# A delta-rule recurrence and a low-rank mixer in one kernel: PSUM as four double banks, regrouped transposes and joins, another load order

## The chip, the cores and the metric

The kernel runs on one core of a Trainium2 chip. The core has a matrix engine (TensorE, PE in the profile), three engines for elementwise work (VectorE or DVE, ScalarE or ACT, GpSimd or POOL), a queue engine for transfers (SyncE or SP) and 16 DMA engines. The metric is the device time of one execution in microseconds. The kernel before takes 720.28 us, the median of three runs (718.12 to 721.35).

## The reference

All data are float32 with 4 batches, 8 heads, 768 steps and head size 48. The first block is the delta rule, one state of 48 x 48 for each batch and head:

```
k_n = k / (norm(k) + 1e-6)
for t in range(S):
    y[t]  = q[t] @ state
    v_old = k_n[t] @ state
    state = state + beta[t] * outer(k_n[t], v[t] - v_old)
```

The eight heads of y are laid side by side (x: 4 x 768 x 384), and the second block is a mixer with rank 32 and an inner width of 1536:

```
u   = x + ((x.T @ U) @ V).T        # over the 768 steps
out = u + relu(u @ w_ch1) @ w_ch2
```

The mixer's inputs U, V, w_ch1 and w_ch2 come as float64.

## The kernel before

**Units and chunks.** The 768 steps are cut into 12 chunks of 64. A unit is six chunks of one batch for all heads, so there are eight units, two to a batch. The data of a unit live in one of two slots in SBUF, so the loads of unit n wait until the recurrence of unit n - 2 has ended (`load`, L252).

**Grams** (`grams`, L359). K and then Q of a unit are transposed on TensorE, two chunks at a time, four transposes into one PSUM bank (`turn`, L367). `products` (L375, L382) multiplies the transposed K with itself and with the transposed Q; the K products are copied by ScalarE (L393), the Q products masked by VectorE (L397).

**Inverse.** Within a chunk the rule needs the inverse of a unit-triangular 64 x 64 matrix. `blocks` (L428) brings the 32 x 32 diagonal blocks into a layout with one block on each partition: unit 0 through TensorE (L465), the others by a round trip through DRAM (L479, L486). There VectorE solves them column by column, with a product (L497) and a subtraction (L503) per column. `split` says whether a block is solved whole (31 columns) or as two halves of 16 (15 columns, twice as many systems at once); units 0 and 1 are split. The result goes back (L522, or L544 and L549). `joins` (L565) puts the blocks together with small matmuls. For a split unit there is an inner join (L579, L598) that joins the halves of 16 to blocks of 32, on all four quarters of 32 rows. The outer join (L621, L638) joins the blocks of 32 to 64, and its matmuls read and write two row quarters. `diagonals` (L652) copies the finished diagonal blocks with GpSimd (L658) and clears the lower ones (L664).

**Recurrence** (`recur`, L673). For each of a batch's 12 chunks: state times K (L704), the first part of y (L715), the right side on VectorE (L725), inverse times right side (L734), a copy z by ScalarE (L743), the state's increment (L749), the second part of y (L759), the new state on VectorE (L772). `put` (L681) copies y to X.

**Weights** (`load_weights`, L801). 27 slices of float64 are loaded as pairs of 32-bit words by GpSimd's queue and turned into float32 by four VectorE instructions and one more on ScalarE (L834 to L862). GpSimd adds and subtracts the halves of w_ch2 (`sums`, L794).

**Mixer.** `front` (L875) computes u for 256 rows, and transposes it (L885, L899, L903, L907). `wide` (L918) does the first layer (L972) with its relu on ScalarE (L928), sums on GpSimd (L944, L951), and the second layer in seven products (L1005), each added to X by VectorE (L957) and stored. There are three such groups to a batch.

**Order.** All parts are Python generators. `run` (L125) is a planner: it keeps a modelled clock for each engine, a modelled state of PSUM and of the loads' landing (`landing`, L106), and emits at each point the ready operation of the highest priority (the second argument of `begin`; a small number is first) that doesn't start more than `HOLD` = 0.15 us after the soonest. The emitted order is each engine's program order. The recurrences of batches 1 to 3 have priority 59, later units' grams and blocks 68 and more, the mixer's matmuls 95. PSUM's eight banks are handed out by name: `pair` has three double banks (0-1, 2-3, 6-7), `one` two single banks (4, 5), and when the mixer starts, 6 and 7 become its two banks `mix` (L921).

## Time and profile before

| | |
|---|---|
| median of the runs | 720.28 us (718.12 to 721.35) |
| the profiled execution | 725.51 us, span 723.7 us |
| TensorE busy, share of the span | 637.3 us, 88% |
| VectorE | 377.1 us, 52% |
| GpSimd | 215.0 us, 30% |
| ScalarE | 182.9 us, 25% |
| mean granted TensorE clock | 0.884 |
| moved by DMA | 44.27 MB, mean 61 GB/s |
| chain that ended last | TensorE 52%, VectorE 29%, DMA 8% of the span |

The profile is of one execution. Busy time is the time in which an engine had at least one instruction under way; matmuls overlap, so the mean duration of one is longer than busy time divided by count. A stage's row gives the stretch, its length, then busy time and instruction count of TensorE, of its weight loads, of VectorE, ScalarE and GpSimd, and at last the granted clock, the DMA share and GB/s. A timeline row gives start, duration, engine, line, operation, operands and count, and in brackets how long the engine had been idle and what it waited for. A group's row gives busy time, the mean of one instruction in ns, and the idle time before. In the lines, `<-` reads "written from".

### The profile page before, as it was taken

What the parts mean: (1) busy time and instruction counts of PE and PEld (TensorE: products, weight loads), DVE (VectorE), ACT (ScalarE), POOL (GpSimd) and SP (SyncE); (2) the same over time, 40 slices, a digit from 0 to 9 for tenths busy, and PEclk for the clock granted to TensorE, in tenths of its full rate; (3) what the DMA queues carried; (4) which work ended last, traced back from release to release, by engine and by line L of the source; (5) the groups of instructions that cost most, each with busy time, mean ns of one, the idle gap of its engine ahead of it and who ended that gap; (6) DMA issues with size and microseconds to landing.
All of it is one profiled execution on the core that took longest, in us unless ns stands there. A gap on an engine that the chain in (4) does not pass through costs nothing.

```text
span 723.7 us, 23375 instructions
## 1 busy us (share of the span) xinstructions
PE 637.3 (88%) x10344; PEld 540.5 (75%) x10344; DVE 377.1 (52%) x925; ACT 182.9 (25%) x399; POOL 215.0 (30%) x281
## 2 busy tenths in 40 slices
PE   5667688659598899999798999999799999999998
PEld 4556576528486688789686887798677887989997
DVE  7577768799958631249678240469494111201001
ACT  3232235325121241331112322421113112020110
POOL 7326341233450250130350511123604302231412
PEclk9965555559798999999979999999799799999999
DMA  9731439852060231342211321521402000000000
GB/s 155 126 92 28 120 84 184 183 125 67 0 122 24 45 73 36 74 88 56 54 36 34 74 56 39 109 48 36 90 24 45 3 24 2 23 0 23 1 23 22
DMA packets 132964, 44.27 MB, mean 61 GB/s; under 512 B 126336, under 2 KB 129408, under 8 KB 132864
## 3 DMA queue, kind: packets, MB, share of 16 engines
q1 hardware_dynamic: 127776, 30.20, 21.2%
q0 software_dynamic: 3488, 12.29, 6.5%
q8 instruction: 81, 1.33, 0.8%
q10 hardware_dynamic: 1600, 0.30, 0.3%
q14 instruction: 19, 0.16, 0.1%
HBM read 32.54 MB, written 10.22 MB: 59 GB/s over the span
## 4 chain that ended last, share of the span: by engine, by line
PE 52%; DVE 29%; DMA 8%; issue 4%; SPq 3%; ACT 1%; POOL 1%; ACTq 0%; DVEq 0%; POOLq 0%
PE P L1005 18%; PE P L972 16%; DVE prod L497 11%; DVE xt L503 10%; PE P L638 2%; PE P L621 2%; SPq L269 2%; PE P L382 2%; DMA slot<-in_q_dram 2%; PE P L899 2%; PE P L367 2%; PE P L734 2%; DMA scr<-xt 2%; DMA wide<-in_moe_w_ch_dram 1%; PE P L704 1%
## 5 line engine op out<-in xcount | busy, mean ns | idle before, releaser
L972 PE MATMUL P<-ut,w_sb 128*128 128x256 f32 x864 | 213.3, 396 | 0.0
L972 PEld LDWEIGHTS P<-ut,w_sb 128*128 128x128 f32 x864 | 161.8, 194 | 24.8 <-issue 0.6
L1005 PE MATMUL P<-w_sb,hs 128*128 128x192 f32 x720 | 129.5, 333 | 0.0
L1005 PEld LDWEIGHTS P<-w_sb,hs 128*128 128x128 f32 x720 | 118.3, 192 | 3.2
L944 POOL TENSOR_TENSOR S<-hs 128x384 f32<-128x384 f32 x24 | 24.7, 1030 | 256.6 <-ACT hs L928 256.6
L957 DVE TENSOR_TENSOR X<-X,P 128x192 f32<-128x192 f32 x84 | 29.5, 351 | 133.4 <-PE P L1005 133.2
L497 DVE TENSOR_TENSOR prod<-gs,xt 128x112 f32<-128x112 f32 (+21 forms) x216 | 86.6, 401 | 6.0
L503 DVE TENSOR_TENSOR xt<-xt,prod 128x112 f32<-128x112 f32 (+21 forms) x216 | 84.2, 390 | 8.0 <-DVE prod L497 0.7
L928 ACT ACTIVATE hs<-P 128x512 f32<-128x512 f32 x72 | 43.0, 597 | 167.6 <-PE P L972 157.5
L1005 PE MATMUL P<-w_sb,S 128*128 128x192 f32 x288 | 56.5, 350 | 5.3 <-POOL S L944 5.3
L1005 PEld LDWEIGHTS P<-w_sb,S 128*128 128x128 f32 x288 | 50.6, 204 | 6.7 <-POOL S L944 5.8
L367 PE MATMUL P<-ident,slot 128*128 128x128 f32 x192 | 37.9, 331 | 9.1 <-DMA slot<-in_q_dram 7.7
L685 ACT COPY X<-P 64x192 f32<-64x192 f32 x96 | 30.1, 314 | 53.4 <-PE P L759 52.8
L658 POOL COPY slot<-zc 32x384 f32<-32x384 f32 x64 | 33.0, 516 | 27.4 <-DVE zc L606 21.3
L382 PE MATMUL P<-slot 48*64 48x64 f32 x1536 | 39.0, 250 | 2.4 <-DVE slot L397 0.7
L382 PEld LDWEIGHTS P<-slot 48*64 48x64 f32 x1536 | 32.6, 159 | 9.6 <-issue 3.4
L743 ACT COPY z<-P 128x192 f32<-128x192 f32 x48 | 15.2, 317 | 89.7 <-PE P L734 89.4
L367 PEld LDWEIGHTS P<-ident,slot 128*128 128x128 f32 x192 | 26.2, 166 | 13.7 <-issue 9.8
L772 DVE TENSOR_TENSOR s<-s,P 128x192 f32<-128x192 f32 x40 | 14.0, 349 | 40.7 <-PE P L749 40.3
L704 PEld LDWEIGHTS P<-s,slot 48*64 48x64 f32 x704 | 16.7, 155 | 24.7 <-DVE s L772 9.4
L734 PEld LDWEIGHTS P<-rhs,slot 64*64 64x64 f32 x704 | 16.9, 155 | 23.3 <-DVE rhs L725 13.1
L734 PE MATMUL P<-rhs,slot 64*64 64x48 f32 x704 | 22.6, 250 | 12.4 <-DVE rhs L725 12.4
(102 smaller groups left out, 769.9 us busy)
## 6 DMA issues: line engine op xcount, KB each, us to landing
wide<-in_moe_w_ch_dram POOLq DMA_DIRECT2D x24, 384.0 KB, 4.0
slot<-in_k_dram SPq DMA_DIRECT2D x84, 72.0 KB
slot<-in_q_dram SPq DMA_DIRECT2D x64, 72.0 KB
out_dram<-X SPq DMA_DIRECT2D x24, 192.0 KB
slot<-in_v_dram SPq DMA_DIRECT2D x48, 72.0 KB
scr<-slot SPq DMA_DIRECT2D x28, 96.0 KB
gs<-scr SPq DMA_DIRECT2D x28, 96.0 KB
scr<-xt SPq DMA_DIRECT2D x28, 96.0 KB
```

The costliest lines, as they stand in the source:

```text
L367: nc.tensor.transpose(p_t[:, c, j], t[:, c0 + c, 2 * j : 2 * j + 2].rearrange("p s d -> p (s d)"), ident)
L382: nc.tensor.matmul(p_g[half(g ^ (par * i)), par, c, j], kq[rows, c0 + c, j, 0, half(g)], kq[rows, c0 + c, j, i, half(g)], start=True, stop ...
L497: nc.vector.tensor_tensor(out=prod, in0=gb[:, :, j : j + 1, j + 1 :].to_broadcast([128, split, m, w]), in1=xb[:, :, 0:m, j : j + 1].to_bro ...
L503: nc.vector.tensor_tensor(out=xb[:, :, 0:m, j + 1 :], in0=xb[:, :, 0:m, j + 1 :], in1=prod, op=ALU.subtract,)
L658: nc.gpsimd.tensor_copy(out=heads(pg[quarter(i)])[:, at, a : a + BK], in_=zc[quarter(i), at])
L685: nc.scalar.copy(x[half(c % 2), c // 2, 4 * D * g : 4 * D * (g + 1)].rearrange("p (j r d) -> p r j d", r=2, d=D), states(p_y)[half(g)],)
L734: nc.tensor.matmul(states(p_c)[half(g ^ par), par, j], zt[half(g), par, cu, j], rhs[half(g), 2 * par + j], start=True, stop=True,)
L928: nc.scalar.activation(hs[:, fs[0] : fs[1] + 1 : fs[1] - fs[0]], p_f, ACTF.Relu)
L944: nc.gpsimd.tensor_tensor(out=to, in0=a, in1=c, op=how)
L957: nc.vector.tensor_tensor(out=to, in0=to, in1=p, op=ALU.add)
L972: nc.tensor.matmul(p_f[:, fs.index(f)], w1_sb[:, t, f * 128 : (f + 1) * 128], ut[:, t], start=(t == 0), stop=(t == KT - 1),)
L1005: nc.tensor.matmul(p_o, a[:, f], w2_sb[:, w, f], start=(first and f == 0), stop=(f == HF - 1), skip_group_check=True,)
```

## The change

- PSUM is handed out as four double banks, `pair` = (0-1, 2-3, 4-5, 6-7); the single banks are gone, and all users take a pair. Banks 6 and 7 still become the mixer's.
- `grams` is two parts, one for K and one for Q, that run apart. A transpose group takes six chunks of one head pair into two banks; products and evictions are by six chunks too. Loads report after each half of the heads.
- The outer join's matmuls use all four row quarters: one head's product sits on the upper, the other's on the lower rows. Their number is the same.
- Units 2 and 3 are split as well (`n < 4`). For unit 2 and later, the diagonal blocks are moved by DMA and not copied by GpSimd: for units 2 and 3 from SBUF, for later ones straight from DRAM. For units 0 and 1, ScalarE takes two of the eight copies.
- The second part of y is its own part, `result`, with a priority just after the recurrence's. z and the state have three buffers each.
- The weights wait for unit 0's seed, the Q load of unit 0 loses its early place, beta is loaded and turned in two parts, the square of the first K goes to GpSimd, and the memsets at the start are divided differently.
- In the planner, the landing is estimated one microsecond later, the starting clocks of VectorE and GpSimd are changed, and priorities under 13 may hold an engine for 0.7 us.

```diff
-    BANK = dict(pair=[0, 2, 6], one=[4, 5], mix=[6, 7])
+    BANK = dict(pair=[0, 2, 4, 6], mix=[6, 7])
...
-        return max(1.9, state["hw"] + 1.4 - state["now"])
+        return max(2.0, state["hw"] + 2.4 - state["now"])
...
-                    hold = HOLD if i[0] < 90 else SWITCH
+                    hold = 0.7 if i[0] < 13 else HOLD if i[0] < 90 else SWITCH
...
+    nc.vector.memset(P[:, :, 0:256], 0.0)
...
-    nc.vector.memset(P[:, 0:4], 0.0)
-    nc.vector.memset(P[:, 4:8], 0.0)
-    nc.vector.memset(gs, 0.0)
+    nc.gpsimd.memset(gs, 0.0)
...
+    nc.gpsimd.memset(zc, 0.0)
...
-        yield need(("rec", n - 2))
+        yield need(("rec", n - 2), *[("x", b - 1, UC * hf + c) for c in range(UC)])
...
+        if n == 0:
+            yield op("pool", 2.1)
+            nc.gpsimd.tensor_tensor(
+                out=ksq, in0=kn[:, :, :, 0:D], in1=kn[:, :, :, 0:D], op=ALU.mult
+            )
...
+        def turn(t, j, i):
+            x = yield op("pe", 0.66, "F", take="pair")
+            p_t = pair(x)[:, :, 0:384].rearrange("p b (c t) -> p b c t", c=3)
+            for c in range(UC):
+                nc.tensor.transpose(
+                    p_t[:, c // 3, c % 3],
+                    t[:, c, 2 * j : 2 * j + 2].rearrange("p s d -> p (s d)"),
+                    ident,
+                )
...
+        def products(j, i):
+            x = yield op("pe", 0.7, "Q", take="pair")
+            p_g = pair(x)[:, :, 0:384].rearrange("p r (c t) -> p r c t", c=UC)
...
-        split = 2 if n < NU else 1
+        split = 2 if n < 4 else 1
...
-                yield op("sp", 0.52)
-                nc.sync.dma_start(
-                    out=zc[quarter(i)], in_=scr2[i].rearrange("q s t -> s q t")
-                )
+                blk, a = scr2[i].rearrange("q s t -> s q t"), BK * (i % 2)
+                if split == 2 or i % 2 == 0:
+                    yield op("sp", 0.52)
+                    nc.sync.dma_start(out=zc[quarter(i)], in_=blk)
+                if split == 1:
+                    yield op("sp", 0.52)
+                    nc.sync.dma_start(out=heads(pg[quarter(i)])[:, :, a : a + BK], in_=blk)
...
                 for g in range(2):
-                    rows = quarter(2 * g + 1)
+                    up, low = quarter(2 * g), quarter(2 * g + 1)
                     nc.tensor.matmul(
-                        p_x[quarter(2 * g), e - 12 * r],
-                        pg[rows, a, c, j, 0:BK],
-                        zc[rows, e],
-                        start=True,
-                        stop=True,
+                        p_x[up, c], pg[low, r, c, 0, 0:BK], below(c, 0, g), start=True, stop=True
+                    )
+                    nc.tensor.matmul(
+                        p_x[low, c], pg[up, r, c, 1, BK:L], above(c, 1, g), start=True, stop=True
                     )
...
                 for g in range(2):
-                    rows = quarter(2 * g)
+                    up, low = quarter(2 * g), quarter(2 * g + 1)
                     nc.tensor.matmul(
-                        p_v[rows, e - 12 * r], zn[rows, e], xz[rows, e], start=True, stop=True
+                        p_v[up, c, 0], above(c, 0, g), xz[up, r, c], start=True, stop=True
+                    )
+                    nc.tensor.matmul(
+                        p_v[up, c, 1], xz[low, r, c], below(c, 1, g), start=True, stop=True
                     )
...
+            if n < NU:
+                for i in range(4):
+                    a = BK * (i % 2)
+                    to, of = heads(pg[quarter(i)])[:, at, a : a + BK], zc[quarter(i), at]
+                    if i < 2 or r == 0:
+                        yield op("pool", 0.5)
+                        nc.gpsimd.tensor_copy(out=to, in_=of)
+                    else:
+                        yield op("act", act(384))
+                        nc.scalar.copy(to, of)
+            elif split == 2:
+                for i in range(4):
+                    a = BK * (i % 2)
+                    yield op("sp", 0.55)
+                    nc.sync.dma_start(
+                        out=heads(pg[quarter(i)])[:, at, a : a + BK], in_=zc[quarter(i), at]
+                    )
+                yield op("sp", 0.0, lat=2.5)
...
+        def result(c, y, z):
+            n, cu = NU * b + c // UC, c % UC
+            _, _, _, qk, _, _, _, _ = units[n]
+            if c == 0:
+                y = yield op("pe", 0.35, "Q", take="pair")
+            else:
+                yield op("pe", 0.35, "Q")
+            p_y = pair(y)[:, :, 0 : 2 * D]
+            for j, par, g in heads:
+                at = half(g ^ par)
+                nc.tensor.matmul(
+                    states(p_y)[half(g), par, j],
+                    qk[at, par, cu, j],
+                    z[at, 2 * par + j],
+                    start=(c == 0 and j == 0),
+                    stop=(j == 1),
+                    skip_group_check=True,
+                )
+            emitted(("y", b, c))
+            yield from put(c, y, p_y)
...
+            yield need(("y", b, c - 3)) if c > 2 else []
             yield op("act", act(192), give=[("pair", xc)])
-            z = small.tile([128, 4, D], FP32, name="z")
+            z = small.tile([128, 4, D], FP32, name="z", bufs=3)
             nc.scalar.copy(z.rearrange("p (r j) d -> p r (j d)", r=2), p_c)
+            begin(result(c, y, z), 2 if b == 0 else 60)
...
+        yield need(("seeded", 0))
         begin(start(0), 22)
...
-        begin(load_beta(), 4)
+        begin(load_beta(0), 12)
+        begin(load_beta(1), 16)
...
-            begin(grams(n), place_of(n))
+            begin(grams(n, 0), place_of(n))
+            begin(grams(n, 1), place_of(n) + 3)
...
-            begin(load(n, "q", (0, 1)), 21 + 4 * n if n else 5)
+            begin(load(n, "q", (0, 1)), 21 + 4 * n)
```

## The prediction

> **What bounds the kernel now.** I read four kinds of view: the page's slices, the busy time by stage, the order of instructions at the stage borders, and the groups with shapes kept apart. The slices (40 of 18.1 us) come first:
>
> ```profile
> PE   5667688659598899999798999999799999999998
> DVE  7577768799958631249678240469494111201001
> PEclk9965555559798999999979999999799799999999
> ```
>
> TensorE is full from about the twelfth slice on. Before that it works in gaps, at half clock, while VectorE carries 5 to 9 tenths. I cut the span where the last product of the first batch's recurrence ends (146.5 us), where the second layer starts (195), and where the last recurrence has ended (610.5). Columns: stretch, its length, busy time of the five engines, granted clock, DMA:
>
> ```profile
> 0.00:146.50 146.50, 101.07 (x3296) 86.73 (x3296) 105.28 (x260) 47.56 (x103) 56.40 (x98) 0.65 0.60 121
> 146.50:195.00 48.50, 31.86 (x231) 23.17 (x227) 46.56 (x86) 15.38 (x28) 20.52 (x19) 0.78 0.26 68
> 195.00:260.00 65.00, 58.37 (x1063) 48.52 (x1063) 42.15 (x115) 14.36 (x37) 20.19 (x28) 0.90 0.28 57
> 260.00:610.50 350.50, 335.96 (x5166) 280.75 (x5164) 169.35 (x431) 91.71 (x208) 89.99 (x113) 0.96 0.24 51
> 610.50:723.70 113.20, 110.02 (x601) 101.31 (x600) 13.80 (x35) 13.93 (x25) 27.93 (x25) 1.00 0.04 15
> ```
>
> From 195 us on TensorE is busy 58.4 + 336.0 + 110.0 = 504.4 us of 528.7: idle 24.3. So the end is the moment S at which the second layer starts, plus TensorE's remaining work, plus its idle time. S is 195 now. What sets S is in TensorE's order of instructions:
>
> ```profile
> 183.20 1.45 PE L899 MATMUL P<-tt,v_sb 128*128 128x384 f32 x4
> 193.66 1.54 PE L907 MATMUL P<-ident,X 128*128 128x128 f32 x6 [9.01 <-DVE X L903]
> 195.00 5.71 PE L1005 MATMUL P<-w_sb,hs 128*128 128x192 f32 x24
> ```
>
> The nine idle microseconds are VectorE's: the addition L903 stands behind the substitution of unit 2 (L497, L503), and so did the weight conversion, whose last piece (L862) ended at 183.6; the weight sums on GpSimd (L798) followed until 191.6. In 140 to 200 us the two substitution lines take 18.3 + 16.4 = 34.7 us of VectorE for this one unit. Unit 1, solved as two half-size systems, took 4.3 + 4.4 = 8.7 between 60 and 140.
>
> The small matmuls, by group:
>
> ```profile
> L638 PE MATMUL P<-xz,zn 32*32 32x32 f32 x768 | 21.1, 219 | 1.9 <-issue 1.0 <-ACT xz L630 0.9
> ...
> L621 PE MATMUL P<-zc,slot 32*32 32x32 f32 x768 | 20.3, 216 | 0.0
> ...
> L598 PE MATMUL P<-xz,zn 32*32 32x16 f32 x384 | 6.7, 210 | 7.4 <-issue 7.4
> ...
> L579 PE MATMUL P<-zc,slot 32*32 32x16 f32 x384 | 6.2, 210 | 1.2 <-issue 1.2
> ```
>
> Busy time over count: 27 ns a record for the joins on two row quarters (L621, L638), 16 to 17 ns for those on four (L579, L598).
>
> [...] the second pair also has half the columns. [...] twelve records of L1005 take 1.95 us alone, 2.15 between tile groups, so 0.2 us for an interleaved group. [...]
>
> ```profile
> 37.12 2.23 DVE L497 TENSOR_TENSOR prod<-gs,xt 128x128 f32<-128x128 f32 x1
> ...
> 37.08 2.12 POOL L354 TENSOR_TENSOR slot<-slot,norm_v 128x1152 f32<-128x1152 f32 x1 [2.05 <-DMA slot<-in_v_dram]
> ```
>
> The first is 0.29 us where GpSimd rests.
>
> **The change, part by part: S.** (1) Units 2 and 3 are solved in halves. Of the 34.7 us of unit 2, 20.5 lay before 184; 8.7 take their place: -11.8 on VectorE before the weights end. Added there: two more transposes (0.56 each) and two corrections L606 (0.42 each): +2.0. (2) One memset of PSUM instead of two (1.77), that of gs (0.94) goes to GpSimd: -2.7. (3) Masks by 384 instead of 256 columns: 18 of 0.417 = 7.5 for units 0 to 2 become 12 at about 0.55 (the 384-column additions of L903) = 6.6: -0.9. Sum of 1 to 3: -13.4. (4) The gather for unit 0 was ready at 27.5, but L474 ran at 30.47, behind the norm of unit 1, whose K landed at 25.5. Weights that load after the seed (15.9 us) leave K1 the queues, and the loads' landing is planned later: -3. The late start of the weights costs nothing: the two pieces converted by 18.8 fit into VectorE's idle time from 18.9 to 26.7, and if they don't, 2.5 us a piece (68.7 us for 27). (5) L903 is no longer behind the long substitution: L1005 follows the sums (191.6) and not 195: -3.4. Together -19.8: **S = 175**. Low end 5 us of gain: if recurrence or loads pace the weights, only (2) and part of the others remain; high end 28, if all 20.5 us leave.
>
> At nothing on this path: the square of K0 on GpSimd (2.1 us by L354, against 1.16 on ScalarE) feeds a factor ready at 15.7, needed at 27.5; the memsets on GpSimd, about 2 us ahead of the beta loads, whose first use is at 9.5, some 4 us after landing; the copies of unit 0 shared by ScalarE and VectorE; two evictions of 768 columns for three of 512 on ScalarE (0.317 us at 192 columns and 0.586 at 512 give 0.80: 1.6 us for 1.76, on an engine a quarter busy); the loads' new wait for the x of the same half a batch earlier, whose products end within a step (under 0.7 us) of the recurrence that they waited for anyway. If that cover goes, each costs its own 1 to 2 us.
>
> **TensorE after S: 504.4.** (a) Unit 2's join (209.0 to 212.4: 3.4) and the rest of unit 3's Q grams (after 200: 3.3) now fall before S, where TensorE idles: -6.7. Unit 2's new inner join lies there too. (b) The outer joins keep their number, 192 records a unit, but alternate over four row quarters, with 192 columns evicted for 384 at the first step. Units 3 to 7 take 25.4 us now; at 16.1 ns they would take 5 x 192 x 0.0161 = 15.5: -9.9. Bounds: nothing, if instruction supply limits it (after bursts at 16 ns the trace shows idle "issue" times of 1.4 to 2.3 us), to -12. (c) Unit 3's inner join: half of 6.2 + 6.7: +6.5. (d) Transposes by six: as many records, but 8 groups a unit for 12; units 4 to 7 save 16 x 0.2 = -3.2. (e) The second y product keeps its place after the state product if both are ready, at no cost; placed alone, 36 x 0.2 = +7.2. I take 0. Sum: 504.4 - 6.7 - 9.9 + 6.5 - 3.2 = **491.1**.
>
> **Idle after S: 24.3.** Unit 3's substitution in 218 to 250 (11.2 + 12.0 us) becomes 8.7, so VectorE frees PSUM sooner: I take 3 off the 6.6 idle between 195 and 260. Two stalls come from GpSimd's memset, queued ahead of the sums L944 and waiting for a DMA:
>
> ```profile
> 359.44 0.98 POOL L445 MEMSET xt<- 128x1056 f32 x1 [11.94 <-DMA scr<-xt]
> ...
> 512.00 0.98 POOL L445 MEMSET xt<- 128x1056 f32 x1 [10.59 <-DMA scr<-xt]
> ```
>
> TensorE waited 5.3 us for L944. The wait stays in the code; the later landing estimate and unit 4's earlier start may move it; I take half, 2.6. Idle: **18.7**, bounds 8 and 30.
>
> GpSimd loses 48 diagonal copies of 0.516 (24.8 us); SP gains 8 issues for units 2 and 3 and 2 for each later one, at about 0.6. Unit 2's now wait on SP for the corrected blocks, and loads and stores stand behind them. SP's loads are 28 x 0.62 = 17 us of some 75 a unit, so 5 us are hidden; uncovered, that unit's next load slips by them. DMA runs at a quarter of its capacity there.
>
> Sum: 175 + 491.1 + 18.7 = 684.8 span. The profiled execution was 1.8 over its span and 5.2 over the median shown, so **about 682 us** in the median's terms.
>
> **What PSUM's new division decides.** Unit 4's last K transposes ran at 268.97, its products at 298.84, right after the recurrence's last step: by the code, the two pairs were in the recurrence's hands.
>
> ```profile
> 268.97 0.66 PE L367 MATMUL P<-ident,slot 128*128 128x128 f32 x4
> ...
> 298.84 0.66 PE L382 MATMUL P<-slot 48*64 48x64 f32 x32
> ```
>
> A third pair lets them in some 30 us earlier. That brings no TensorE time by itself, but recurrences must stay ahead: after the last one (about 608) 98 us of its own front and mixer remain (113.2 less 15.2 of the batch before, by the counts left). For an end at 685 it must end by 587, 20 earlier; the shift of S and the third pair give that.
>
> **Rivals.** B, *the start doesn't move and the joins gain nothing*: S = 190, TensorE 504.4 - 6.7 + 6.5 = 504.2, idle 24.3: 718.5 span, 715; with (e) 722. So about 719. For it: DMA waits of 0.4 to 0.7 us before several conversions, issue gaps. Against: 46.6 us of VectorE in the 48.5 before S.
>
> C, *slower: three shared pairs instead of two pairs and two single banks*. y may hold a pair into the next step, and joins, transposes and fronts now claim whole pairs. If each of the 36 later recurrence steps waits 2 us for one, the last ends at 587 + 72 = 659, and 98 later the kernel: 757 span, **754**. It decides from 627 on, that is 40/36 = 1.1 us a step. Against: a step lasts 6.0 us now, three groups with a mixer piece of 1.5 to 2.15 us between, so a pair has time to come free.
>
> **How the numbers follow.** Forecast 0.70 (own range 664 to 710: S from 167 to 190, joins and idle at their bounds), B 0.10, C 0.20, from 724 (1.1 us a step) up. 0.5% (3.6 us) is about what a measurement can tell from no change. Faster: 0.69 of the forecast and 0.03 of B, 0.72; same 0.07; slower 0.21. The range 662 to 732 leaves out the ends of the forecast and most of C.
>
> **What would show it.** L497 with L503 for units 2 and 3 near 8.7 us each; the first L1005 near 175; L621's and L638's successors at 16 ns; products of unit 4 inside the recurrence of batch 1; last recurrence before 587; TensorE idle below 20 after S. Wrong if the first L1005 is at 190 or later, if waits for PSUM evictions grow in the recurrence, or if the last 98 us start after 627.

## The result, and the profile after

The changed kernel takes **751.2 us** (median of 4 runs, 750.3 to 753.8) against 720.8 us before (4 runs, 718.1 to 725.5): **1.042 times the time before, 95% interval 1.036 to 1.048**. Forecast were 682 us, with 662 to 732 as the range. The profiled execution spans 750.4 us (723.7 before, which was the slowest of its four runs, so that the difference of the spans, 26.7 us, is smaller than that of the medians, 30.4). The ratios in this text leave out runs in a slow state (over 1.5% above the fastest of their kernel) and the medians don't, which matters only for a_first below (median 720.0 without them, 721.4 with them).

The page's slices of the changed kernel, 40 of 18.8 us (busy tenths of TensorE and VectorE, granted TensorE clock):

```profile
PE   5856769694669778997778889978999999999998
DVE  4738666994763396339829623872220110101001
PEclk9997555996559799999897899989999999999999
```

TensorE is full only from the twenty-ninth slice on. In the fifteen slices before that it has six digits of 7 and five of 8; the kernel before had five such digits in all between the twelfth slice and the last but one. The stages, cut at the same events as in the prediction (last product of the first batch's recurrence, first product L1059 of the second layer, then 65 us, then the end of the last recurrence; columns: stretch, length, busy time of the five engines, granted clock, DMA):

```profile
0.00:131.40 131.40, 92.87 (x3252) 82.01 (x3254) 81.46 (x214) 43.53 (x95) 52.65 (x89) 0.75 0.53 111
131.40:220.10 88.70, 57.88 (x1414) 46.38 (x1410) 70.55 (x166) 26.93 (x56) 31.11 (x33) 0.73 0.48 106
220.10:285.00 64.90, 56.29 (x1215) 48.94 (x1212) 34.57 (x80) 14.94 (x32) 12.94 (x14) 0.90 0.35 68
285.00:570.00 285.00, 247.18 (x4303) 205.61 (x4302) 144.10 (x343) 70.58 (x162) 51.82 (x56) 0.93 0.26 53
570.00:750.40 180.40, 176.59 (x944) 160.53 (x942) 19.86 (x51) 23.53 (x41) 45.08 (x41) 1.00 0.04 14
```

The first batch's recurrence is done 15 us earlier (131.4 for 146.5), and then the second layer starts 25 us later (220.1 for 195). After it TensorE is busy for 56.3 + 247.2 + 176.6 = 480.1 us of 530.3: idle 50.2 where 24.3 were before and 18.7 were forecast. Over the whole span it was busy for 637.3 us before and 630.8 after, so idle for 86.4 and 119.6: **6.5 us less work, 33.2 us more standing still**.

What stands ahead of the second layer is seen in the order of VectorE's and TensorE's instructions (start, duration, operation, and in brackets the idle time ahead of it with what ended it):

```profile
174.11 1.02 DVE L580 STREAM_TRANSPOSE zn<-zc 128x384 f32<-128x384 f32 x2
184.55 0.42 DVE L626 SCALAR_TENSOR_TENSOR zc<-P,upper_rows,zc 128x192 f32<-128x192 f32 x1 [9.41 <-PE P L618]
...
174.72 1.72 PE L601 MATMUL P<-zc,slot 32*32 32x16 f32 x147
178.24 0.78 PE L601 MATMUL P<-zc,slot 32*32 32x16 f32 x43 [1.81 <-issue]
...
184.03 1.52 PE L618 MATMUL P<-xz,zn 32*32 32x16 f32 x100 [3.88 <-issue]
...
216.70 0.68 PE L768 MATMUL P<-s,slot 48*64 48x48 f32 x16 [2.98 <-DVE s L825]
...
220.10 1.33 PE L1059 MATMUL P<-w_sb,hs 128*128 128x192 f32 x3
```

This is unit 2's inner join, which the change adds (L601 and L618; L579 and L598 before). TensorE runs 147 of its matmuls in 1.72 us, then waits 1.81 us for nothing that the profile shows ("issue"), and later 3.88 us more. VectorE's correction L626 waits 9.41 us for it, and the last weight conversions stand behind the correction, mixed there with unit 3's substitution and steps of the second recurrence: the last of them (L916; L862 before) ends at 211.9, not at 183.6.

The joins by group, shapes kept apart (busy us and mean ns, then idle time ahead of them with its cause):

```profile
L618 PE MATMUL P<-xz,zn 32*32 32x16 f32 x768 | 12.9, 209 | 11.8 <-issue 11.8
L651 PE MATMUL P<-zn,slot 32*32 32x32 f32 x384 | 12.4, 219 | 2.1 <-issue 2.1
L666 PE MATMUL P<-xz,zn 32*32 32x32 f32 x384 | 12.1, 212 | 3.7 <-issue 1.9 <-ACT xz L656 1.7
L601 PE MATMUL P<-zc,slot 32*32 32x16 f32 x768 | 11.7, 199 | 7.9 <-issue 7.9
L648 PE MATMUL P<-zc,slot 32*32 32x32 f32 x192 | 7.4, 238 | 1.9 <-issue 1.9
```

The inner joins have twice the records (1536 for 768) and 19.7 us of idle issue time ahead of them where they had 8.6. The outer joins L648 to L669 interleave, so that the busy times of their groups overlap: counting each matmul only for time that no earlier one covers, they take 22.9 us for 36.5 before, with 10.4 us of idle time for 1.9.

The same count by kind of work shows where the 33 us of idle time lie. Idle time is put to the matmul that ended it. The transposes of beta and of unit 0's blocks are left out (10 to 12 us busy, 6 to 10 idle in these runs), and about 3 us at the two ends of the span are in no row. Recurrence includes the second y product.

| TensorE, us: busy + idle ahead of it | before | after | a_split | a_first4 | a_first |
|---|---|---|---|---|---|
| inner joins | 12.1 + 8.6 | 21.9 + 19.7 | 11.7 + 11.4 | 22.1 + 18.5 | 11.4 + 8.1 |
| outer joins | 36.5 + 1.9 | 22.9 + 10.4 | 21.5 + 8.6 | 21.8 + 5.4 | 20.6 + 6.8 |
| recurrence | 86.6 + 26.6 | 94.6 + 41.5 | 85.2 + 23.2 | 92.3 + 36.6 | 87.7 + 29.7 |
| transposes and products of grams | 68.9 + 11.5 | 65.4 + 8.3 | 65.1 + 9.5 | 61.8 + 10.0 | 61.9 + 11.3 |
| mixer's fronts | 34.8 + 20.1 | 38.7 + 28.3 | 37.9 + 14.4 | 37.7 + 10.4 | 36.5 + 7.3 |
| factors (L342, L355 after) | 2.0 + 2.8 | 1.6 + 0.6 | 1.9 + 30.9 | 1.4 + 0.0 | 1.8 + 5.4 |
| both layers of the mixer | 384.7 + 5.3 | 374.9 + 0.0 | 373.7 + 1.5 | 382.7 + 21.5 | 381.1 + 21.1 |

The three columns on the right are experiments told below: units 2 and 3 whole; unit 2 behind the weights, in halves; the same, whole.

### The profile page after: what moved, and what is told of

It reads as the page before. It is cut to its first block, busy times and chain, and to the rows that moved or that the text cites. A ratio compares the mean times of both kernels' runs of the same rounds, so it can differ in the third digit from the quotient of the medians.

```text
span 750.4 us, 24865 instructions
## 1 busy us (share of the span) xinstructions
PE 630.8 (84%) x11112; PEld 543.5 (72%) x11112; DVE 350.5 (47%) x852; ACT 179.5 (24%) x385; POOL 193.6 (26%) x232
## 4 chain that ended last, share of the span: by engine, by line
PE 55%; DVE 24%; issue 7%; SPq 5%; DMA 5%; ACT 2%; POOL 1%; DVEq 0%; ACTq 0%; POOLq 0%
PE P L1059 21%; PE P L1026 16%; DVE prod L519 8%; DVE xt L525 7%; SPq L272 3%; PE P L379 2%; PE P L405 2%; PE P L797 2%; DMA scr<-slot 2%; PE P L953 1%; PE P L601 1%; SPq L501 1%; DMA slot<-in_v_dram 1%; PE P L961 1%; DVE s L825 1%
## 5 line engine op out<-in xcount | busy, mean ns | idle before, releaser
L1026 PE MATMUL P<-ut,w_sb 128*128 128x256 f32 x864 | 204.2, 391 | 0.0
L1059 PE MATMUL P<-w_sb,hs 128*128 128x192 f32 x720 | 130.1, 337 | 0.0
L1059 PEld LDWEIGHTS P<-w_sb,hs 128*128 128x128 f32 x720 | 121.5, 196 | 3.0 <-issue 1.2
L1011 DVE TENSOR_TENSOR X<-X,P 128x192 f32<-128x192 f32 x84 | 29.7, 353 | 165.3 <-PE P L1059 165.2
L998 POOL TENSOR_TENSOR S<-hs 128x384 f32<-128x384 f32 x24 | 24.5, 1020 | 240.3 <-ACT hs L982 240.3
L519 DVE TENSOR_TENSOR prod<-gs,xt 128x30 f32<-128x30 f32 (+20 forms) x184 | 77.6, 422 | 4.8
L525 DVE TENSOR_TENSOR xt<-xt,prod 128x30 f32<-128x30 f32 (+20 forms) x184 | 71.8, 390 | 6.3
L1059 PE MATMUL P<-w_sb,S 128*128 128x192 f32 x288 | 51.5, 334 | 0.0
L1059 PEld LDWEIGHTS P<-w_sb,S 128*128 128x128 f32 x288 | 48.0, 194 | 0.6
L379 PE MATMUL P<-ident,slot 128*128 128x128 f32 x192 | 34.6, 338 | 6.3 <-DVE ct L239 5.5
L768 PE MATMUL P<-s,slot 48*64 48x48 f32 x704 | 23.3, 257 | 18.7 <-DVE s L825 15.6
L807 ACT COPY z<-P 128x192 f32<-128x192 f32 x48 | 15.3, 318 | 98.0 <-PE P L797 88.1
L957 DVE TENSOR_TENSOR X<-X,P 128x384 f32<-128x384 f32 x24 | 12.9, 551 | 52.9 <-PE P L953 52.4
L405 PE MATMUL P<-slot 48*64 48x64 f32 x1536 | 35.4, 251 | 2.0 <-issue 1.0
L768 PEld LDWEIGHTS P<-s,slot 48*64 48x64 f32 x704 | 17.5, 162 | 25.9 <-DVE s L825 19.7
L1005 POOL TENSOR_TENSOR hs<-hs,S 128x768 f32<-128x768 f32 x12 | 21.8, 1814 | 49.1 <-PE P L1059 49.1
```

Source lines behind the costliest of these rows:

```text
L379: nc.tensor.transpose(p_t[:, c // 3, c % 3], t[:, c, 2 * j : 2 * j + 2].rearrange("p s d -> p (s d)"), ident,)
L405: nc.tensor.matmul(p_g[half(g ^ (par * i)), par, c], kq[rows, c, j, 0, half(g)], kq[rows, c, j, i, half(g)], start=True, stop=True,)
L519: nc.vector.tensor_tensor(out=prod, in0=gb[:, :, j : j + 1, j + 1 :].to_broadcast([128, split, m, w]), in1=xb[:, :, 0:m, j : j + 1].to_bro ...
L525: nc.vector.tensor_tensor(out=xb[:, :, 0:m, j + 1 :], in0=xb[:, :, 0:m, j + 1 :], in1=prod, op=ALU.subtract,)
L768: nc.tensor.matmul(states(p_b)[half(g), par, j], kq[half(par, D), cu, j, 0, half(g)], states(s_old)[half(par, D), g, j], start=True, stop= ...
L998: nc.gpsimd.tensor_tensor(out=to, in0=a, in1=c, op=how)
```

## The experiments

I had three theories. **W**: the weights' loads, held back by the change, set the start of the second layer. **J**: solving units 2 and 3 in halves costs more on TensorE, in their inner joins, than it saves on VectorE. **P**: PSUM as equal pairs lets other work in ahead of the path. Two more came up on the way: **O**, that the order which the planner writes is itself worth what was being measured, and the theory of the prediction itself, that an earlier second layer ends the kernel earlier. All ratios are to the kernel before, in runs on the same chip (its medians there were 721 to 724 us). The last two columns are from one profiled execution each. It lies within 0.6% of the median, except before (725.5), a_first (716.6) and b_hold (723.1).

| Run | what it is | median us | ratio, 95% interval | first second-layer product | TensorE busy + idle of its span |
|---|---|---|---|---|---|
| before | | 720.8 | 1 | 195.0 | 637.3 + 86.4 |
| after | the change | 751.2 | 1.036 to 1.048 | 220.1 | 630.8 + 119.6 |
| a_weights | after, loads not held back | 746.9 | 1.023 to 1.039 | 216.1 | 630.4 + 115.1 |
| b_late | before, loads held back | 724.1 | 0.998 to 1.003 | 186.6 | 634.6 + 87.8 |
| a_split | after, units 2 and 3 whole | 720.7 | 0.991 to 0.996 | 212.3 | 607.5 + 112.2 |
| b_split | before, units 2 and 3 in halves | 742.7 | 1.017 to 1.032 | 212.0 | 654.9 + 88.2 |
| a_split3 | after, unit 3 whole | 730.4 | 1.009 to 1.015 | 216.0 | 622.8 + 109.2 |
| a_thin | after, inner joins thinned | 740.6 | 1.022 to 1.037 | 213.8 | 617.0 + 120.0 |
| b_pairs | before, PSUM as pairs | 738.2 | 1.017 to 1.029 | 193.7 | 631.8 + 106.7 |
| b_joins | before, joins on four quarters | 725.7 | 1.001 to 1.007 | 193.7 | 617.7 + 106.3 |
| b_plan | before, new planner constants | 738.2 | 1.020 to 1.029 | 181.8 | 634.9 + 102.6 |
| b_hold | before, hold 0.20 | 729.0 | 1.005 to 1.013 | 189.7 | 629.2 + 92.1 |
| b_land | before, landing + 0.1 | 723.0 | 0.999 to 1.003 | 194.7 | 637.0 + 84.2 |
| a_hold4 | after, hold 0.4 for 0.7 | 736.4 | 1.016 to 1.026 | 229.5 | 629.0 + 106.0 |
| a_after | after, joins of 2, 3 behind the weights | 736.4 | 1.018 to 1.028 | 212.1 | 624.1 + 114.4 |
| a_split_w | a_split and loads not held back | 730.9 | 1.007 to 1.013 | 200.8 | 613.7 + 117.7 |
| a_split_plan | a_split, old constants | 727.2 | 1.005 to 1.011 | 184.8 | 608.5 + 115.9 |
| a_split_norm | a_split, factors first | 721.9 | 0.999 to 1.003 | 215.8 | 605.8 + 114.2 |
| a_first4 | after, all of unit 2 behind the weights | 748.8 | 1.031 to 1.042 | 170.6 | 631.2 + 115.2 |
| a_first | the same, units 2 and 3 whole | 721.4 | 0.992 to 0.998 | 164.1 | 611.8 + 103.1 |

### The weights' loads: undone, and done alone

```diff
-        yield need(("seeded", 0))      # a_weights: taken out of the change
         begin(start(0), 22)
+        yield need(("seeded", 0))      # b_late: put into the kernel before
```

> The changed kernel with the weights' loads no longer held back until unit 0 is seeded. Theory W (weights start too late, so the last conversion, 211.9 us, and with it the first L1059, 220.1 us, came late): the last L915 falls to about 185, the first second-layer product to about 192, the time to 722 (715 to 730). Theory J (the inner joins of units 2 and 3 stop TensorE for want of instructions and VectorE behind it) and theory P (PSUM as equal pairs lets other work in ahead): the loads were not what paced the weights; first second-layer product still after 212, time 742 to 752.

> The kernel before with the weights' loads held back until unit 0 is seeded, nothing else. Theory W: first L1005 10 to 25 us later (205 to 220), time 730 to 745. Theory J and the prediction (a late start costs nothing, or 2.5 us a piece for two pieces): first L1005 at 195 to 200, time 718 to 726.

Undone, the ratio falls from 1.042 to 1.031, with intervals that overlap, and the second layer still starts at 216.1. Done alone, nothing is lost (724.1 against 724.1). W falls, and with it the worry of the prediction that late loads cost 2.5 us a piece. In b_late the second layer even starts 8.4 us earlier (186.6 for 195.0), and the kernel is no faster.

### Units 2 and 3 in halves: undone, and done alone

```diff
-        split = 2 if n < 4 else 1
+        split = 2 if n < NU else 1     # a_split (NU = 2); b_split the other way; a_split3: n < 3
```

> The changed kernel with units 2 and 3 solved whole again. Theory J: VectorE's waits for L618 (20.2 us before the second layer, 9.4 of them in one wait at 175 to 184) shrink to units 0 and 1, the first L1059 comes at 195 to 203, time 725 to 733. Theory W: the substitution grows back by some 12 us of VectorE ahead of the second layer and nothing is won: first L1059 at 218 or later, time 748 to 765. Theory P: near no change, 742 to 756.

> The kernel before with units 2 and 3 solved in halves, nothing else. The prediction's part (1) alone: VectorE ends the weights some 10 us earlier, first L1005 at 183 to 187, time 710 to 716. Theory J: the inner joins cost more than the halving saves: first L1005 at 198 or later, time 724 to 740.

> The changed kernel with unit 3 solved whole and unit 2 in halves. If the price lies in both inner joins alike, about half of the 30 us of solving both whole is won: 732 to 738. If it lies in unit 2's, ahead of the second layer: 743 to 752, first L1059 near 220. If it lies in unit 3's, which would bring the batch's recurrence ahead of the second layer: 719 to 727.

Without the halves the changed kernel takes 720.7 us: 30.5 us less than with them, and 0.7% less than the kernel before. (There the edit also sends the diagonal blocks of units 2 and 3 straight from DRAM and not from SBUF; what that alone is worth was not run. b_split doesn't have this: GpSimd copies its diagonal blocks either way.) Put into the kernel before alone, the halves cost 2.4%, 18.6 us. So **the halves cost time in both directions**, as J has it, and by more than J forecast (725 to 733 and 724 to 740): the part of the change that the prediction credited most is the one that loses the time. With unit 3 whole the kernel takes 730.4 us, 20.8 less than with both in halves, and with unit 2 whole as well 9.8 less again. The first lies between two of the forecasts. In the run of before with halves, TensorE's busy time grows by 17.6 us and its idle time by 1.8; the groups of the inner joins (count, busy us and mean ns, idle):

```profile
L598 PE MATMUL P<-xz,zn 32*32 32x16 f32 x768 | 12.3, 201 | 10.6 <-issue 10.6
L579 PE MATMUL P<-zc,slot 32*32 32x16 f32 x768 | 10.7, 196 | 3.3 <-issue 3.3
```

With 384 records each they took 6.7 and 6.2 us with 7.4 and 1.2 idle. But the starts that J expected were wrong: with whole units the second layer still begins at 212.3, later than before, and the kernel is faster all the same.

### Fewer matmuls in the same order

```diff
-                    for i in range(4):
+                    for i in range(4) if n < NU or e % 6 == 0 else ():     # both inner products
```

> The changed kernel with five sixths of the inner joins' matmuls of units 2 and 3 left out (320 of 384 records a unit, so the output of these units isn't the reference's); evictions, corrections, waits and the order on every engine stay. If the number of small instructions is the price (their time on TensorE and the idle issue time in the bursts): the inner joins fall from 21.9 us busy and 19.7 idle to about 13 and 12, first L1059 at 208 to 212, time 728 to 737. If the price is the order of the work (VectorE held in line behind the correction, the recurrence ahead of the second layer): 744 to 752.

This keeps the order on TensorE, VectorE, ScalarE and GpSimd as in the changed kernel. The inner joins fall to 13.4 us busy and 9.7 idle, 18.5 less than the 41.6 of the changed kernel; the time falls by 10.7 us (the ratio from 1.042 to 1.030; the intervals touch at their ends, and one of the four runs took 748.2), while the recurrence waits longer (41.5 us idle to 52.5). The time, 740.6, lies between the two forecasts. The thinned groups:

```profile
L618 PE MATMUL P<-xz,zn 32*32 32x16 f32 x448 | 7.9, 208 | 4.7 <-issue 4.0 <-ACT xz L610 0.7
L601 PE MATMUL P<-zc,slot 32*32 32x16 f32 x448 | 7.8, 206 | 5.0 <-issue 5.0
```

So the number of small instructions is a cause, worth some 10 of the 30 us in this order. The other two thirds aren't shown by this run.

The stops go with the queue of instruction loads on the page of the changed kernel (packets, MB, share):

```profile
q8 instruction: 87, 1.43, 0.8%
```

87 packets of 16,384 bytes for 11,112 matmuls with their weight loads are 128 pairs a packet. The kernel before has 81 for 10,344; 768 more matmuls are 6 more packets. By the trace's DMA records the packets started at 175.8, 181.3 and 185.8, and took 0.9 to 1.4 us; TensorE went on at 178.2, 184.0 and 188.1, each time 1.3 to 1.5 us after a packet's end. These three stops stand 127 and 128 matmuls apart, one packet's share. Around unit 3's inner join (243.2 to 252.7) packets came at 240.0, 245.0, 249.0, 253.4 and 257.2: 128 pairs each 4.3 us, **34 ns a matmul**, where a burst took 12 ns (147 in 1.72 us).

### PSUM and the outer joins, each alone

b_pairs: the list of banks of the change, and every claim of a single bank made one of a pair. b_joins: the change's new outer joins in the kernel before (even heads as they were, odd ones from the other row quarters, 192 columns evicted at the first step, a pair of banks claimed at the second); the core of its first step:

```diff
-                        p_x[quarter(2 * g), e - 12 * r],
-                        pg[rows, a, c, j, 0:BK],
-                        zc[rows, e],
+                        p_x[up, c], pg[low, r, c, 0, 0:BK], below(c, 0, g), start=True, stop=True
+                    )
+                    nc.tensor.matmul(
+                        p_x[low, c], pg[up, r, c, 1, BK:L], above(c, 1, g), start=True, stop=True
```

> The kernel before with PSUM as four (later three) equal double banks, each claim of a single bank taking a double one, nothing else. Rival C of the prediction (shared pairs make the recurrence wait, 1 us and more a step): 740 or more. If the division of PSUM costs nothing: 714 to 724.

> The kernel before with only the outer joins on all four row quarters. Step (b) of the prediction, 9.9 us off for five units, 16 us a kernel on TensorE in all: 706 to 713. If instruction supply takes half of it back (10 us of idle issue time in the changed kernel's outer joins against 1.9): outer joins 22 busy and 8 to 10 idle, time 711 to 718. If order decides: 718 or more.

Pairs alone cost 2.3% (738.2 us, between the two forecasts): TensorE's busy time is 5.5 us less, its idle time 20.3 us more, most of it ahead of the recurrence (26.6 to 33.9), the factors (2.8 to 11.7) and the fronts (20.1 to 24.1). Rival C's size was nearly reached, but not in its way: 7.3 us more over the 48 steps of the recurrence are 0.15 us a step, not 1.1.

The joins do on TensorE most of what step (b) said: 22.8 us busy for 36.5, so 13.7 of the 16 less, but 8.8 idle for 1.9; in all TensorE is busy for 19.6 us less. The kernel doesn't become faster: 725.7, a little slower. Idle time rose by 19.9 us: by 6.9 ahead of the joins themselves, 7.8 ahead of the grams' transposes and products (19.3 for 11.5), 3.1 ahead of the fronts and 3.0 ahead of the recurrence. So half of what the joins save is lost again on the joins, and the rest in idle time elsewhere. The rows of the grams' products, before and in that run:

```profile
L382 PE MATMUL P<-slot 48*64 48x64 f32 x1536 | 39.0, 250 | 2.4 <-DVE slot L397 0.7 <-ACT slot L373 0.6 <-ACT X L685 0.6
L382 PE MATMUL P<-slot 48*64 48x64 f32 x1536 | 39.7, 248 | 11.5 <-ACT slot L373 5.5 <-DVE slot L397 2.0 <-issue 1.9
```

and the wait of the fronts' transposes for VectorE's addition (us in total, times, longest):

```profile
PE P L907 <- DVE X L903: 12.4, 3, 9.0
PE P L915 <- DVE X L911: 14.5, 5, 9.3
```

Each of the two edits also makes the planner write another order, and each brought 20 us of idle time, spread over many parts of the kernel. That made order itself the suspect.

### Order alone

```diff
-    SWITCH, HOLD = 0.15, 0.15
+    SWITCH, HOLD = 0.15, 0.2                                      # b_hold
-        return max(1.9, state["hw"] + 1.4 - state["now"])
+        return max(1.9, state["hw"] + 1.5 - state["now"])         # b_land
-                    hold = 0.7 if i[0] < 13 else HOLD if i[0] < 90 else SWITCH
+                    hold = 0.4 if i[0] < 13 else HOLD if i[0] < 90 else SWITCH    # a_hold4
```

b_plan: the kernel before with the four constants of the change.

> The kernel before with only the planner's four constants of the change (start of two clocks, hold 0.7 for the early units, landing 1 us later): every engine does the same instructions in another order. If the order written by the planner is worth 10 us and more by itself: outside 713 to 731. If order alone is cheap: 717 to 727.

> The kernel before with one constant of the planner, the hold, 0.20 for 0.15: the same instructions, in an order that differs in some 360 lines on TensorE. If the order as such is worth 10 us and more, and the one of before is a good one: 730 to 742. If what the edits of the change cost has other causes than the new order that each brings: 718 to 726.

> The kernel before with the planner's landing 0.1 us later: the same instructions, with a handful of neighbours swapped. A control of the run with the other hold: 718 to 726 by every theory, unless four swaps alone can cost 10 us.

> The changed kernel with the hold of the early units 0.4 for 0.7: the same instructions in another order. If the order of the changed kernel is a bad one among those that the planner might write: 735 to 746. If its loss lies in its instructions, PSUM and inner joins: 747 to 755.

These runs have the same instructions as the kernel they come from. The new constants cost the kernel before 2.4%, another hold 0.5 to 1.3% (729.0 us, in neither forecast), and a landing of 0.1 us more, which swaps a handful of neighbours, nothing. Another hold takes 14.9 us off the changed kernel. So O holds: **in these runs an order is worth up to 15 us in either direction**, and part of what the change lost belongs to the order that its constants and costs made the planner write. The cost of the pairs alone (15 us over the runs beside it) is not larger than that and can't be told from it, nor can the split between unit 2 and unit 3 be taken as exact. The price of the halves stands out: 30.5 and 18.6 us above, and some 27 in a third pair of orders below (a_first4 and a_first), always of one sign and each more than 15.3 us, the most that a reordering alone did here.

### Moving the stall, and the start of the second layer

```diff
+            yield need(("block", n, r), *([("sums", 0), ("sums", 3)] if NU <= n < 4 else []))   # a_after
+            begin(norms(n), place_of(n) if n < NU else 36)                                   # a_split_norm
+            yield need(("c", n), ("returned", n - 1),
+                       *([("sums", 0), ("sums", 3)] if n == NU else []))                   # a_first, a_first4
```

> The changed kernel with the joins of units 2 and 3 planned only once all weight sums are made. Theory O (order: two thirds of the split's price are VectorE and GpSimd held in line behind unit 2's joins, with the weights behind them): no L618 wait of 9.4 us ahead of the second layer, first L1059 at 190 to 203, time 728 to 738. If the price comes from what the joins and the batch's recurrence take anywhere: first L1059 earlier but the time stays at 742 to 754, the joins' busy and issue time (22 and 20 us) now after it.

> The changed kernel with units 2 and 3 whole and the weights' loads not held back. Without the inner joins in the way TensorE still stood 22.8 us behind the factors of unit 3 (L355, ahead of the first second-layer product at 212), which VectorE made behind substitution and weights. If earlier loads let VectorE end the weights earlier: first L1058 at 195 to 205, time 703 to 714. If the loads pace nothing: 717 to 724.

> The changed kernel with units 2 and 3 whole and the planner's four constants as before. Without order effects 716 to 725, as with the new constants (720.7). If the constants cost what the 22.8 us stand-still behind unit 3's factors suggests: 698 to 712. If they help: 728 to 740.

> The changed kernel with units 2 and 3 whole, and the norms and factors of units 2 to 7 planned with a priority ahead of the weights: TensorE no longer stands 22.8 us behind unit 3's factors. If that stall is what keeps the gain of the rest of the change (29.8 us of TensorE's busy time less than before): 698 to 710. If the stall only moves to the next in line: 716 to 726.

The run a_after came out at 736.4, as theory O had it, but not by its mechanism: the second layer began at 212.1, since now a join stood 26.8 us in front of it, waiting for a transposition that VectorE did behind the weights. In a_split it was the factor of unit 3, with that edited in a_split_norm a join of unit 2. TensorE's first row in the list of waits of a_after (us in total, times, longest):

```profile
PE P L618 <- DVE zn L580: 26.8, 1, 26.8
```

of a_split:

```profile
PE P L355 <- DVE ct L346: 30.9, 4, 22.8
```

and of a_split_norm:

```profile
PE P L648 <- DMA slot<-scr: 27.4, 1, 27.4
```

The stall goes to the next instruction of units 2 and 3 that the planner had put ahead of the second layer, since on the chip the results come later than planned. Earlier loads (a_split_w) moved the start to 200.8 and made the kernel 10 us slower; the old constants (a_split_plan) moved it to 184.8, and it was 6.6 us slower. Neither time lies in any range forecast for it. The last pair then took all of that work behind the weights:

> The changed kernel, units 2 and 3 in halves, but unit 2's substitution (and so its joins and the batch's recurrence) planned behind the weights on every engine. If the loss is mainly the work of units 2 and 3 standing on VectorE, GpSimd and TensorE ahead of the second layer: first L1059 at 180 to 195, time 716 to 730; the inner joins' records (10 us by the run with thinned joins) stay. If the loss lies after the second layer's start: first L1059 as early, time 738 to 752.

> The same with units 2 and 3 whole: TensorE's busy time near 608 as in the other run with whole units, and none of the idle 20 to 35 us ahead of the first second-layer product, where TensorE stood behind unit 2's join or unit 3's factors: first L1059 at 180 to 195, time 694 to 708. If the stall only moves behind that product (batch 1's recurrence comes later and its front is waited for): 714 to 726.

The first second-layer product comes 49.5 us earlier in a_first4 than in the changed kernel (min/median/max ns, first and last start):

```profile
L1059 PE MATMUL P<-w_sb,hs x720: 326/326/689, 170.6 to 742.9; 128*128 128x192 f32 x180
```

and the time is 748.8 us against 751.2. TensorE then waits for the last weights instead (15.6 us in three waits), runs 7.9 us in the 29.4 up to 200, and the batch's recurrence, the joins and their waits come after. The same with whole units takes 721.4 us. So two things are settled. **The start of the second layer doesn't set the end**: starts of 187 (b_late), 195 (before) and 212 (a_split) end at 724, 721 and 721, and one of 182 (b_plan) at 738; the starts of 164 and 171 in the last pair, after which TensorE first waits, end at 721 and 749. And **the halves cost some 27 us here too**, where they lie behind the weights: of the 31.5 us between the spans 21.1 are the inner joins' (10.7 busy, 10.4 idle), 11.5 the recurrence's, by the table above. By the same rows the changed kernel has 18.5 and 27.7 us more than a_split there, 14.7 more for the fronts, and 30.6 less for the factors, where a_split had its stall. Why the recurrence waits longer with the halves was not tried apart; the inner joins' own part is what the thinned run supports.

No version beat both kernels by more than the 0.7% of a_split.

## Why the prediction was wrong

**What bounds the kernel** was written as a sum: the start S of the second layer, plus TensorE's remaining work, plus its idle time. The sum holds for the result too (220.1 + 480.1 + 50.2 = 750.4). Against the forecast S came 45 us late (220.1 for 175), the idle time was 31.5 us longer (50.2 for 18.7), and the remaining work 11.0 us shorter (480.1 for 491.1), since more of it now lies ahead of S. What the sum doesn't say, and the prediction took for granted, is that a microsecond won on S is won at the end; b_late and b_plan, with S at 187 and 182, show that it isn't. Up to S VectorE did 151.8 us of work before and 152.0 after: what the halves freed was filled with unit 3's substitution and with steps of the second recurrence, and VectorE's idle time went from 43.2 to 68.1 us.

**S, step (1), the halves of units 2 and 3**: the substitutions did shrink (L519 and L525 take 9.0 us for unit 2 and 12.0 for unit 3, for 34.7 of unit 2 before; 8.7 forecast). **The step that failed is the price of the new inner joins.** Unit 2's was put at nothing on TensorE (it "lies there too", in idle time) with 2.0 us on VectorE, and unit 3's at 6.5 us, its busy time alone. In the changed kernel the two take 20.9 us more of TensorE, 9.8 busy and 11.1 waiting for instructions; VectorE's correction waits 9.4 us in one piece for unit 2's, with the last weights behind it. Put as a sum: the forecast gave the halves -11.8 + 2.0 on S, +6.5 on TensorE and -3 idle, about -6; alone they cost 18.6 us, in the change 30.5. The inner joins account for 14 to 21 us of that. The rest differs from order to order: the recurrence takes 27.7 us more in the changed kernel than in a_split and 11.5 more in a_first4 than in a_first, but 0.4 in b_split, where the outer joins take 6.7. The prediction had these at nothing, and their cause stays open. **Steps (2) and (3)** can't be told apart in the runs. **(4)**, late weights at no cost, held (b_late), but the 3 us that it was to bring aren't seen at the end. **(5)**, the product following the sums: in the changed kernel the sums (L851) end at 216.3 and the first product comes at 220.1, so that the sums, too, are late. The last step of the sum, 684.8 to "about 682", gives 681.4 with the +1.8 and -5.2 that it names; nothing hangs on it.

**TensorE.** (b), the outer joins: forecast -9.9 for five units, so 15.8 for eight, an estimate that took over the 16 ns of the inner joins, which have half the columns; measured for eight -13.6 us busy, but +8.5 idle, of which most is issue time: 5.1 won. Of the bounds given, "instruction supply limits it" was the one to look into: the trace of before already had 81 packets of instructions. (c), the inner join: 6.5 us a unit forecast, for one of the two units; measured for two 14.3 (b_split), 18.5 (a_split) and 21.1 (a_first), busy and idle, so 7 to 10 a unit. (d), groups by six: -3.2 forecast for units 4 to 7, -3.5 measured on the transposes and products of all units (68.9 to 65.4). (e), the second y product at no cost: held as far as the runs go; with units 2 and 3 whole, recurrence and y are busy for 85.2 us for 86.6 (94.6 in the changed kernel). Work over the span fell by 6.5 us, and by 29.8 with units 2 and 3 whole, of which 11 are the mixer's own matmuls, 1872 in both. The granted clock after S was 0.98 in that run and 0.96 before; whether that makes all of the 11 isn't shown.

**Idle after S**: forecast 18.7, measured 50.2. The two stalls at the sums L998 (5.3 us) did go, all of them; what was not foreseen is what came instead. TensorE's longest waits after 220 in the changed kernel (us in total, times, longest):

```profile
PE P L961 <- DVE X L957: 12.5, 5, 8.4
PE P L768 <- DVE s L825: 9.3, 12, 3.4
PE P L953 <- DVE tt L945: 5.4, 1, 5.4
```

Fronts and recurrence wait for VectorE, which at the three longest of the fronts' waits (ending at 360, 423 and 494) is doing the whole-block substitutions of later units.

**The rivals.** C named 754 us, and 751 was measured, but not by its mechanism, so the nearness is luck: the last recurrence step's first product ran at 561, well before 627 and 587, and some 185 us of the mixer followed, where 98 were counted. Of the recurrence's waits only one looks like C's, 4.0 us of L778 for L680, an eviction that by the code frees a pair. PSUM's part alone cost 15 us, within what order alone does; whether the pairs or the order make those 15 us stays open. B, for which start and joins stay as they are, has no run that speaks for it: start and joins both moved.

**The signs.** The start at 190 or later was named as the mark of failure, and it came. But the marks of success came too, apart from the start and the idle time: substitutions near 8.7 us, the last recurrence step before 587, outer joins at 15 ns a record in busy time (22.9 us for 1536; 16 forecast), and unit 4's products inside the recurrence of batch 1: they start at 232.9, between its steps up to 217 and those from 262, 66 us earlier than before. With the pairs alone (b_pairs) they also ran inside it, at 279.7. None of these was proof of a gain.

What stays open: how the 15 us that another order gives back in the changed kernel divide among its constants, PSUM and costs; why the recurrence waits more with the halves; and whether any order of this change would use the 30 us that TensorE has less to do with whole units.

## What to carry to other kernels

Price a burst of small matmuls by the instructions it needs as well as by its busy time, and ask who is in line behind its result: here the inner joins of two units cost 14 to 21 us of TensorE where 6.5 were counted. When a planner writes the order, run controls that only reorder before crediting a part of a change with 10 us; here a constant moved by 0.05 was worth some 6. An earlier start of the last stage is no gain unless the sum of TensorE's busy and idle time falls with it.

## What the runs showed of the hardware

- The changed kernel had 87 instruction packets of 16,384 bytes for 11,112 matmuls with weight loads, the kernel before 81 for 10,344: 128 matmuls a packet in both. In and around the inner joins of units 2 and 3 of the changed kernel one came each 3.8 to 5.5 us, 4.3 on average at unit 3's, 34 ns a matmul, and TensorE stood 1.6 to 3.9 us between bursts, the fastest of 12 ns a matmul. For the outer joins, of whose 10.4 us of idle time there 8.1 are "issue", four row quarters won little over two: 33.3 us with their waits for 38.4, 21.7 ns a matmul for 25.0.
- Over 200 to 300 us the granted clock was 0.98 in a_first, which has no inner join there, and 0.81 in a_first4, which has two, at nearly the same busy time of TensorE (92.4 and 90.9 us). First a_first, then a_first4:

```profile
200.00:300.00 100.00, 92.44 (x1696) 79.46 (x1695) 56.56 (x154) 25.83 (x60) 21.24 (x26) 0.98 0.30 62
200.00:300.00 100.00, 90.88 (x2116) 80.11 (x2116) 36.46 (x103) 20.75 (x48) 15.58 (x20) 0.81 0.35 69
```

  In the changed kernel it was 0.82 there: 0.50 up to 223.3 and from 247.2 to 257.4, and 1.00 between the two. What lowered it isn't shown. Over the whole kernels the recurrence is busy for 92.3 us in a_first4 and 87.7 in a_first; that the clock makes the difference isn't shown.
